# Loading the second row tile of x in two halves on two DMA queues: a change to the first microseconds of a long kernel

## The chip, the cores and the metric

The kernel runs on one core of one Trainium2 chip. The metric is device time in microseconds (us), lower is better. Before the change it was 921.45 us (median of three runs, 920.68 to 922.20). The profile of one execution gives a span from the first to the last instruction, here 919.1 us. The time of a run is longer than its span by what lies outside the instructions. The spans of most other runs are on record too, without a profile.

## The reference

One layer of a transformer, in bfloat16: normalise, sliding-window attention against cached keys and values, a SwiGLU network as a gate, and a residual.

```
x = A_x                                   # 1 x 2048 x 640
xn = _layernorm(x, axis=-1)
s = _A_ref(xn, A_k_cache, A_v_cache, A_wq, A_wo)      # 32 heads of 192, window of 512 keys
g = _silu(_B_ref(xn, B_w_gate, B_w_up, B_w_down))     # 640 -> 1536 -> 640
return x + s * g
```

## The kernel before

Only the opening matters here. The rows of x are worked on in tiles of 128. The first four tiles are normalised on VectorE and transposed on TensorE, each while TensorE multiplies the tile before it by the first three column blocks of the gate and up weights. From the fourth tile on TensorE has dense work, and the other 900 us follow.

The loads are issued from two queues, SP (`nc.sync`) and ACT (`nc.scalar`):

```python
def load_x(t, engs=(nc.sync,)):
    x_t[t] = lnx.tile([P, D], bf, name="x_t")
    n = P // len(engs)
    for k, eng in enumerate(engs):
        r = slice(k * n, (k + 1) * n)
        eng.dma_start(out=x_t[t][r, :], in_=x2[t * P + r.start : t * P + r.stop, :])
...
load_x(0, (nc.scalar, nc.sync))
load_x(1, (nc.scalar,))
load_first(slice(0, 2), (nc.sync, nc.scalar))     # gate on SP, up on ACT: input blocks 0, 1
load_first(slice(2, NC))                          # the rest of both, blocks 2 to 4, on SP
load_x(2, (nc.scalar,))
nc.scalar.activation(act_t[:], one_t[:], ACT.Sqrt)
load_x(3)
load_gu(1)
```

`load_first` loads 384 columns of the gate and of the up weights; I call its first part the first gate and up weights (192 KB each) and its second part the remaining ones (288 KB each). A row tile of x is 160 KB.

Two details of the order of work matter. While the loads are under way TensorE runs matmuls on zeros (`keep_warm`), which stand ahead of the real work in its queue until about 5.7 us. And the statistics of a tile are interleaved with the normalisation of the tile before it:

```python
ln_stats(0)
ln_sqrt(0)
ln_stats(1, lambda: ln_apply(0, (slice(0, 2 * P), slice(2 * P, D))))
ready(0)
...
            if k == len(order) * 7 // 10 and t < 3:
                if t < 2:
                    ln_stats(t + 2, lambda: ln_apply(t + 1))
                ...
                ready(t + 1)
```

`ln_stats(t, between)` calls `between` after the first half of tile t's statistics, so tile t - 1 is normalised only when tile t has landed. `ready` does the transposes. Of the matmuls of tile 0, the first part uses the gate weights only, then come the transposes of tile 1, then the remaining up weights.

The softmax here doesn't subtract the row's maximum and nothing guards it: scores larger than these inputs give would overflow.

## Time and profile before

| | before |
|---|---|
| median of 3 runs, us | 921.45 |
| span of the profiled run, us | 919.1 |
| TensorE busy | 914.2 us, 99% of the span |
| share of TensorE in the chain that ended last | 99% |
| start of the first dense matmuls, on tile gu | 14.38 us |

The last row is the yardstick. After it TensorE hardly stops, so whatever the opening gains or loses shows as a shift of that start: 919.1 - 14.38 = 904.7 us remain.

### The profile page before, as it was taken

What the parts mean: (1) busy time and instruction counts of PE and PEld (TensorE: products, weight loads), DVE (VectorE), ACT (ScalarE), POOL (GpSimd) and SP (SyncE); (2) the same over time, 40 slices, a digit from 0 to 9 for tenths busy, and PEclk for the clock granted to TensorE, in tenths of its full rate; (3) what the DMA queues carried; (4) which work ended last, traced back from release to release, by engine and by line L of the source; (5) the groups of instructions that cost most, each with busy time, mean ns of one, the idle gap of its engine ahead of it and who ended that gap; (6) DMA issues with size and microseconds to landing.
All of it is one profiled execution on the core that took longest, in us unless ns stands there. A gap on an engine that the chain in (4) does not pass through costs nothing.

```text
span 919.1 us, 23174 instructions
## 1 busy us (share of the span) xinstructions
PE 914.2 (99%) x9920; PEld 548.9 (60%) x9920; DVE 601.8 (65%) x844; ACT 473.9 (52%) x840; POOL 85.2 (9%) x269
## 2 busy tenths in 40 slices
PE   9999999999999999999999999999999999999998
PEld 6444444465757575656565656566666666665665
DVE  6443321467677777777777777676867777777657
ACT  4222222557464646565656565655555555556471
POOL 0000000000000000000000000000000000001976
PEclk9999999999999999999999999999999999999999
DMA  9412430045352534253534343435243444443525
GB/s 299 79 35 64 92 82 0 1 75 112 54 113 50 111 51 108 54 108 54 108 58 109 57 108 52 110 53 108 56 87 73 90 77 75 91 71 102 120 59 166
DMA packets 248167, 77.53 MB, mean 84 GB/s; under 512 B 228993, under 2 KB 248065, under 8 KB 248065
## 3 DMA queue, kind: packets, MB, share of 16 engines
q1 hardware_dynamic: 245696, 73.39, 38.9%
q10 hardware_dynamic: 2368, 2.67, 0.9%
q8 instruction: 77, 1.26, 0.6%
q14 instruction: 26, 0.20, 0.1%
HBM read 38.93 MB, written 2.62 MB: 45 GB/s over the span
## 4 chain that ended last, share of the span: by engine, by line
PE 99%; DMA 1%; DVE 0%; ACTq 0%; issue 0%
PE mm L448 22%; PE sc L462 18%; PE mm L487 16%; PE sc L602 15%; PE sc L282 11%; PE mm L312 6%; PE sc L572 4%; PE sc L564 2%; PE mm L539 2%; PE mm L564 1%; DMA x_t<-in_A_x_dram 1%; PE gu L282 0%; PE mm L321 0%; PE sc L487 0%; PE sc L539 0%; PE mm L462 0%
## 5 line engine op out<-in xcount | busy, mean ns | idle before, releaser
L466 ACT ACTIVATE p_t<-sc 128x1024 bf16<-128x1024 f32 x254 | 252.9, 1022 | 120.5 <-PE sc L462 120.5
L453 DVE TENSOR_REDUCE qT<-mm 128x512 bf16<-128x1024 f32 x189 | 231.1, 1223 | 99.0 <-PE mm L448 96.5
L517 ACT ACTIVATE O_b<-mm,r 128x192 bf16<-128x192 f32 x486 | 164.6, 421 | 183.7 <-issue 136.9
L448 PE MATMUL mm<-xnT,wq_p 64*128 64x512 bf16 x1890 | 237.5, 376 | 0.0
L462 PE MATMUL sc<-qT,khat 64*128 64x512 bf16 x1524 | 198.0, 376 | 0.0
L487 PEld LDWEIGHTS <-p_t 64*128 64x128 bf16 x3584 | 159.3, 93 | 33.8
L487 PE MATMUL mm<-V_p,p_t 64*128 64x193 bf16 x3520 | 176.7, 242 | 0.0
L615 DVE TENSOR_TENSOR s_m<-s_m,sc 128x1024 f32<-128x1024 f32 x108 | 131.9, 1221 | 60.7 <-PE sc L602 52.3
L602 PE MATMUL sc<-wo_p,OT_b 64*128 64x512 bf16 x1296 | 168.8, 376 | 0.0
L448 PEld LDWEIGHTS <-wq_p 64*128 64x128 bf16 x1890 | 105.0, 94 | 98.9 <-issue 0.8
L462 PEld LDWEIGHTS <-khat 64*128 64x128 bf16 x1536 | 85.3, 94 | 80.4 <-DVE s_t L615 0.3
L602 PEld LDWEIGHTS <-OT_b 64*128 64x128 bf16 x1296 | 70.1, 94 | 44.1 <-issue 0.3
L615 DVE TENSOR_TENSOR s_t<-s_t,sc 128x512 f32<-128x512 f32 x108 | 74.2, 687 | 28.4 <-PE sc L572 26.6
L589 POOL MEMSET turn_t<- 128x1 f32 x220 | 21.6, 98 | 700.2 <-PE mm L487 506.2
L290 DVE TENSOR_TENSOR hT<-sc,sg 128x512 bf16<-128x512 f32 x46 | 31.7, 692 | 81.5 <-ACT sg L289 81.5
L289 ACT ACTIVATE sg<-sc 128x512 bf16<-128x512 f32 x46 | 27.3, 596 | 69.8 <-PE sc L282 69.8
L282 PE MATMUL sc<-xnT,wu_sb 128*128 128x512 bf16 (+1 forms) x260 | 60.5, 355 | 0.0
L282 PE MATMUL sc<-xnT,wg_sb 128*128 128x512 bf16 (+1 forms) x260 | 60.3, 355 | 0.1
L572 PE MATMUL sc<-OT_b,wo_p 64*128 64x512 bf16 (+1 forms) x345 | 50.3, 376 | 0.0
L312 PE MATMUL mm<-wd_sb,hT 128*128 128x512 bf16 x192 | 43.9, 379 | 0.0
L282 PEld LDWEIGHTS <-wu_sb 128*128 128x128 bf16 x285 | 27.2, 98 | 26.8 <-issue 0.2
L282 PEld LDWEIGHTS <-wg_sb 128*128 128x128 bf16 x285 | 27.2, 98 | 26.3
(83 smaller groups left out, 418.8 us busy)
## 6 DMA issues: line engine op xcount, KB each, us to landing
wo_p<-in_A_wo_dram SPq DMA_DIRECT2D x16, 480.0 KB, 4.8
K_p<-in_A_k_cache_dram SPq DMA_DIRECT2D x32, 192.0 KB, 4.6
V_p<-in_A_v_cache_dram SPq DMA_DIRECT2D x32, 192.0 KB, 3.6
wq_p<-in_A_wq_dram SPq DMA_DIRECT2D x64, 80.0 KB, 2.9
wq_p<-in_A_wq_dram SPq DMA_DIRECT2D x16, 160.0 KB, 3.2
x_t<-in_A_x_dram SPq DMA_DIRECT2D x13, 160.0 KB, 3.2
x_b<-in_A_x_dram SPq DMA_DIRECT2D x4, 512.0 KB, 6.4
OT_b<-O_b SPq DMA_TRANSPOSE x124, 2.8
```

The source lines that it names most:

```text
L282: nc.tensor.matmul(out, w_sb[:, c, f * P : (f + 1) * P], xnT[:, c, qc], start=(c == 0), stop=(c == NC - 1),)
L290: nc.vector.tensor_tensor(hTs[b][:, f, :], u, sg[:], ALU.mult)
L312: nc.tensor.matmul(dn, at, by, start=(f == 0), stop=(f == NF - 1))
L448: nc.tensor.matmul(q_ps[:, h, :], pairs[pr]["wq"][r, c, j * P : (j + 1) * P], xnT[r, c, b * 512 : (b + 1) * 512], start=(c == 0), stop=(c ...
L453: nc.vector.reduce_sum(qTs[i][:, j, :], q_ps[:, :, :].rearrange("p h n -> p n h"), axis=AX.X)
L462: nc.tensor.matmul(sc[:, h, :], khat[r, j, ks], qT[r, j, :], start=(j == 0), stop=(j == 2))
L466: nc.scalar.activation(p_t[:, :, :], sc[:, :, :], ACT.Exp, scale=scale)
L487: m = nc.tensor.matmul(acc[:, k, h * 256 : h * 256 + Dh + 1], Ps[i][kc][r, h, qt * P : (qt + 1) * P], V_p[r, kc, h, 0 : Dh + 1], start=(p ...
L517: nc.scalar.activation(O_b[:, qt, h, :], a_k[:, h, 0:Dh], ACT.Copy, scale=r[:, k, h, :])
L572: nc.tensor.matmul(ps.rearrange("p (t q) -> p t q", q=P), pairs[i // NB]["wo"][r, j, MC:D], OTs[i][:, :, :].rearrange("p (t j) q -> p j t ...
L602: m = nc.tensor.matmul(ps[:, k, :], OTs[i][r, 3 * (2 * half + k) + j, :], pairs[i // NB]["wo"][r, j, MAIN], start=(turn == 0 and j == 0), ...
L615: nc.vector.tensor_tensor(to, to, ps, ALU.add)
```

## The change

The intent: tile 1 of x should arrive sooner, so that VectorE, and after it TensorE, can begin sooner.

```diff
         load_x(0, (nc.scalar, nc.sync))
-        load_x(1, (nc.scalar,))
+        load_x(1, (nc.scalar, nc.sync))
         load_first(slice(0, 2), (nc.sync, nc.scalar))
```

ACT then loads rows 0 to 63 of the tile and SP rows 64 to 127, ahead of the gate weights.

## The prediction

> **What bounds the kernel now.** I read the page from the top: busy time of each engine, then the chain that ended last, then that chain in order of time over the first 20 us (the only part that the change can touch), then the engines' timeline there.
>
> ```profile
> PE 914.2 (99%) x9920; PEld 548.9 (60%) x9920; DVE 601.8 (65%) x844; ACT 473.9 (52%) x840; POOL 85.2 (9%) x269
> ...
> PE 99%; DMA 1%; DVE 0%; ACTq 0%; issue 0%
> ```
>
> TensorE carries 99% of the chain, and its span is 919.1 us. All that is not TensorE work lies before the first dense matmuls. A change to the order of the first loads can at most win what the chain spends outside TensorE there. The chain in order of time shows how much that is (start, length, what):
>
> ```profile
> 1.33 0.59 ACTq L188
> 1.92 0.03 issue
> 1.95 0.45 ACTq L193
> 2.40 0.03 issue
> 2.43 4.79 DMA x_t<-in_A_x_dram
> 7.22 0.02 issue
> 7.24 0.49 DVE stats L243
> 7.74 0.07 DVE rstd L265
> 7.81 0.03 issue
> 7.83 0.46 DVE xn L267
> 8.29 0.05 issue
> 8.34 0.45 PE tp L335 x5
> ```
>
> So the start is bound by a load of x that is issued at 2.43 and lands at 7.22 us. By the order of the issues that is row tile 2, the fourth transfer of the ACT queue, not row tile 1, which the change splits. From 8.34 us on there is only TensorE in the chain. What row tile 1 itself costs is in VectorE's timeline (start, length, instruction, and in brackets the idle time before it):
>
> ```profile
> 4.87 0.49 DVE L243 BATCH_NORM_STATS2 stats<-x_t 128x6 f32<-128x320 bf16 x1 [0.29 <-DMA x_t<-in_A_x_dram]
> 5.28 0.15 DVE L265 RECIPROCAL rstd<-rstd 128x1 f32<-128x1 f32 x1
> 5.46 0.64 DVE L267 TENSOR_SCALAR xn<-x_t,mv,rstd 128x256 bf16<-128x256 bf16 x2
> ...
> 7.24 0.49 DVE L243 BATCH_NORM_STATS2 stats<-x_t 128x6 f32<-128x320 bf16 x1 [0.50 <-DMA x_t<-in_A_x_dram]
> ...
> 9.13 0.49 DVE L243 BATCH_NORM_STATS2 stats<-x_t 128x6 f32<-128x320 bf16 x1 [0.21 <-DMA x_t<-in_A_x_dram]
> ```
>
> There are three waits on x: 0.29 us for row tile 1, 0.50 for row tile 2, 0.21 for row tile 3. The first matters although row tile 0 is already there, because in program order the first half of tile t+1's statistics stands before the normalisation of tile t: tile 0 is held up by tile 1's load, tile 1 by tile 2's, tile 2 by tile 3's. TensorE's weight loads show what of this reaches it:
>
> ```profile
> 5.86 0.13 PEld L335 LDWEIGHTS <-xn 128*128 128x128 bf16 x2 [0.23 <-DVE xn L267]
> ...
> 8.33 0.28 PEld L335 LDWEIGHTS <-xn 128*128 128x128 bf16 x5 [0.23 <-DVE xn L267]
> ...
> 10.25 0.21 PEld L335 LDWEIGHTS <-xn 128*128 128x128 bf16 x3
> ```
>
> It waits 0.23 us before the transposes of tile 0 and 0.23 before those of tile 1. Before those of tile 2 (10.25) it has no wait to speak of, but little room either: in VectorE's timeline the normalised tile 2 is written from 9.73 to 9.73 + 0.45 = 10.18, only 0.07 earlier.
>
> **What the Trainium skill says.** "DMA: Bandwidth & Descriptors", section "Rules for kernel authors", says of two transfers to disjoint partition halves "Don't bother", because both use the same 16 engines. The trace can't refute that: in the issues of the first 0.7 us the two 80 KB halves of tile 0 landed after 2.3 and 2.6 us, the whole 160 KB of tile 1, behind one of them, after 3.5. The gain, if any, has to come from the order in the two queues and not from bandwidth. The same page, "Queues, rings and completion order", says that each DMA engine takes turns between the queues for which it has work. I use that below; the trace fits it loosely, for ACT's 592 KB in four transfers were all landed at 7.22 us while SP had also been served. "TensorE: Matmul & The Clock Gate", Part 1, says that the array starts at half clock and is released after a window of sustained work whose phase does not depend on the kernel, 107 ns against 56 ns between small matmuls. The trace agrees: weight loads for the first matmuls start at 6.78, 6.88, 6.99, 7.10, 7.20, 7.28 and from there 7.34, 7.39, 7.45, 7.50, that is 0.11 us apart and then 0.055. The full clock comes at about 7.28 us. The page's warning that this moment shifts from run to run would be a noise of some tenths of a microsecond; one trace can't show it.
>
> **The change part by part.** One 160 KB load on ACT becomes two of 80 KB, one on each queue. ACT issues as many as before (tile 0's half, tile 1's half instead of the whole, weights, tile 2). SP issues one more, before its first weights: SP's other half of tile 0 took 0.59 us to issue, so everything after it on SP is issued some 0.5 to 0.6 us later. No instruction of another engine is added or removed, and no byte: ACT's share of the opening falls from 80 + 160 + 192 + 160 = 592 KB to 512, SP's rises by 80.
>
> To say when something lands I count the bytes in front of it. In the stretches from 4.2 to 8.2 us the DMA moved 306, 316, 322 and 341 GB/s with its engines about fully busy, so 80 KB fewer in one's own queue, with the other queue taking equal turns, is some 160 KB fewer in all, or 160 x 1.024 / 320 = 0.51 us. Estimates, all from this trace:
> - Tile 1 lands now at 4.87 - 0.04 = 4.83 us. Its two halves, each second in its queue, should land at about 4.1. VectorE is free for it at 4.37 + 0.21 = 4.58, so the wait of 0.29 us goes and nothing takes its place there. Tile 0's normalised columns come 0.29 earlier, at about 5.5.
> - TensorE's transposes of tile 0 gain 0.23 us at most (its own wait), or somewhat less, since the warming matmuls before them end at about 5.7. The first real matmuls move from 6.72 to about 6.5. They then run at half clock until 7.28, so 0.2 us earlier is two matmuls more by then, worth 2 x 0.056 = 0.11 us.
> - Tile 2 has 80 KB fewer before it on ACT: 7.22 - 0.5 = 6.7 us. Its statistics can start at about 6.75 in place of 7.24, so normalised tile 1 is there at about 7.85 in place of 8.28, and TensorE's second wait of 0.23 goes. Together with the 0.11 TensorE is up to 0.3 us ahead at about 8 us.
> - The gate and up weights of the first two blocks: ACT's 192 KB come earlier; SP's land now at 1.37 + 4.3 = 5.67, and with 80 KB more before them at about 6.2. TensorE loads them at 6.34 now and would at 6.15. No wait, or 0.05. The rest on SP: gate at about 2.2 + 5.1 = 7.3, used at 7.56; up at 2.75 + 5.5 = 8.25, used at 8.57. For the up weights all 1,440 KB of both queues lie in front before and after, so they still land at about 8.25, just when a TensorE 0.3 us ahead would ask for them.
> - Tile 3, on SP: 3.27 + 5.8 = 9.07 us. In front of it and with it are 1,600 KB before and after the change, whatever the queue. It does not come earlier. Its statistics start at 9.13 as now, tile 2 is normalised at 10.18 as now, and the transposes of tile 2 can't begin before about 10.23. They begin at 10.25 now.
>
> So the 0.3 us that TensorE is ahead at 8 us is handed back at 10.2, in a wait for tile 2 which has no counterpart now. Sum: -0.11 - 0.23 + 0.28 = -0.06 us. After that every matmul follows the one before, and 0.05 us on the way stays 0.05 us at the end. Some straggling packets may well move by 0.1, so I take -0.1 us: 921.45 - 0.1 = 921.35.
>
> **The rivals.**
> First, the whole 0.3 us stays, because tile 3 comes earlier too. For it: with ACT's queue empty sooner SP runs alone for longer, and the stretch 8.2 to 9.2 us with SP alone moved 368 GB/s against 306 to 322 with both. Against it: the bytes are the same. It would make 921.1.
> Second, the weights become the bound: SP issues 0.5 to 0.6 us later, and from 3.2 to 4.2 us the engines were only 0.83 busy (202 GB/s), so the backlog isn't full there and a later issue may leave a gap. The first gate weights would hold the first matmuls to about 6.5 to 6.8, and the up weights land at 8.5 to 8.8. TensorE would then lose 0.2 to 0.3 us, with nothing after to win it back: 921.7. Against it: the added half of tile 1 fills just that gap on SP.
> Third, it is hidden altogether, since keep-warm matmuls stand in TensorE's queue to about 5.7 us: 921.45.
>
> **Range and chances.** All these lie within 0.3 us, or 0.03%. The three runs of before span 920.68 to 922.20, so the noise is larger than any of the effects, and it sets the range: 920.4 to 922.2. For 2% the change would need 18 us, while all waits on x in the opening sum to 1.0 us. Faster by over 2%: 0.01; within 2%: 0.98; slower by over 2%: 0.01.
>
> **What would show it.** Right: no wait of VectorE before the first statistics of tile 1 and a start near 4.58; first real matmul near 6.5; tile 2's load landing near 6.7; a new wait of 0.2 to 0.3 us before TensorE's transposes of tile 2; and start times of the dense matmuls (14.38 and 17.10 in the chain now) earlier by 0.0 to 0.1. Wrong: those starts earlier by 0.3, tile 3 landing well away from 9.07, or a wait for weights at 6.5 or 8.3 us. The prediction as a time fails only if the run-to-run noise is larger than three runs show.

## The result, and the profile after

The changed kernel took 920.96 us (median of six runs, 920.64 to 924.69), the kernel before 921.33 (median of six, 920.45 to 922.20). The ratio of the fast runs is 1.0004 with a 95% interval of 0.9987 to 1.002: the same (within 2%). A ratio here is the mean time of one kernel's fast runs over that of the other's in the same rounds, so it isn't quite the ratio of the medians: here the 924.69 pulls the mean up. Executions over 1.5% slower than the fastest of the same kernel are left out of the means.

The profiled execution happened to be that 924.69, with a span of 922.9 us. From its page, busy time and chain:

```profile
PE 914.9 (99%) x9920; PEld 551.6 (60%) x9920; DVE 601.7 (65%) x844; ACT 473.7 (51%) x840; POOL 85.2 (9%) x269
...
PE 98%; DMA 1%; SPq 0%; DVE 0%; issue 0%
```

TensorE's busy time is 0.7 us more than before, while the span is 3.8 us more. The chain in order of time (start, length, what) says where the rest is:

```profile
3.39 7.15 DMA wu_sb<-in_B_w_up_dram
10.53 0.05 issue
10.58 0.28 PE sc L282 x2
```

The chain no longer runs through tile 2 of x, but through the remaining up weights, which were issued at 3.39 and landed at 10.53 us. TensorE's weight loads in the same stretch (idle time and what ended it in brackets):

```profile
6.45 0.10 PEld L282 LDWEIGHTS <-wg_sb 128*128 128x128 bf16 x1 [0.41 <-DMA wg_sb<-in_B_w_gate_dram]
...
7.48 0.51 PEld L282 LDWEIGHTS <-wg_sb 128*128 128x128 bf16 x9 [0.36 <-DMA wg_sb<-in_B_w_gate_dram]
7.94 0.32 PEld L335 LDWEIGHTS <-xn 128*128 128x128 bf16 x5
10.58 0.51 PEld L282 LDWEIGHTS <-wu_sb 128*128 128x128 bf16 x9 [2.32 <-DMA wu_sb<-in_B_w_up_dram]
```

The transposes of tile 1 begin at 7.94 (8.33 before) and have no wait ahead of them any more. Three waits for weights are new: 0.41, 0.36 and 2.32 us. After the last of them the weight loads go at 11.13, 11.24, 11.35, 0.11 us apart, and stay at that pace to 14.4 us. The clock record of this trace says why: half the clock was granted from 11.04 us on for 3.41 us, and the view by stretches gives 0.52, 0.50 and 0.50 for 11 to 12, 12 to 13 and 13 to 14 us (the other profiles of this section and of the table below have no such stretch between the opening and the end). At half pace 3.41 us cost an estimated 1.7, so nearly half of the 3.8 us is the clock after the late load, and not the wait itself. VectorE's statistics of tiles 1, 2 and 3:

```profile
4.59 0.49 DVE L243 BATCH_NORM_STATS2 stats<-x_t 128x6 f32<-128x320 bf16 x1
...
6.38 0.44 DVE L243 BATCH_NORM_STATS2 stats<-x_t 128x6 f32<-128x320 bf16 x1
...
11.04 0.49 DVE L243 BATCH_NORM_STATS2 stats<-x_t 128x6 f32<-128x320 bf16 x1 [2.79 <-DMA x_t<-in_A_x_dram]
```

The waits for tiles 1 and 2 are gone, and one of 2.79 us for tile 3 has come. So this trace shows what the change was meant to do and a loss many times larger; yet four of the other five runs were at or under 921.05. One profile doesn't tell what belongs to the change and what to the run. The experiments had to settle that first.

### The profile page after: what moved, and what is told of

Its sections match the earlier page's. It is cut to its first block, busy times and chain, and to the rows that moved or that the text cites. A ratio compares the mean times of both kernels' runs of the same rounds, so it can differ in the third digit from the quotient of the medians.

```text
span 922.9 us, 23176 instructions
## 1 busy us (share of the span) xinstructions
PE 914.9 (99%) x9920; PEld 551.6 (60%) x9920; DVE 601.7 (65%) x844; ACT 473.7 (51%) x840; POOL 85.2 (9%) x269
## 3 DMA queue, kind: packets, MB, share of 16 engines
q10 hardware_dynamic: 2304, 2.59, 0.9%
## 4 chain that ended last, share of the span: by engine, by line
PE 98%; DMA 1%; SPq 0%; DVE 0%; issue 0%
PE mm L448 22%; PE sc L462 18%; PE mm L487 16%; PE sc L602 15%; PE sc L282 11%; PE mm L312 6%; PE sc L572 4%; PE sc L564 2%; PE mm L539 2%; DMA wu_sb<-in_B_w_up_dram 1%; PE mm L564 1%; PE gu L282 0%; PE mm L321 0%; PE sc L487 0%; PE sc L539 0%; SPq L188 0%
```

## The experiments

Two theories. A (chance): in each execution some load is late, whichever kernel it is; the late up weights are such a case. B (the change): the extra transfer on SP makes SP's later loads late. And one question behind both: in which order do the DMA engines serve what the two queues have issued?

### Repeats of both kernels

No edit; each run gives one more profile and five more times.

> The changed kernel, not altered, profiled a second time. Theory A (chance): the 2.3 us in which TensorE waited for the remaining up weights in the first profile was one late transfer, not a property of the change; now the up weights land near 8.3 us, the wait for them is under 0.3 us, the span is near 919 us and the first dense matmul on tile gu (14.38 us in the chain of the kernel before) starts between 14.1 and 14.5. Theory B (the change pushes SP's weights too late): the wait for the up weights is there again, at least 0.5 us, and the span is at least 920 us. Time ratio to the kernel before under A 0.9995 to 1.0000, under B 1.001 to 1.003.

> The kernel before, not altered, against itself: how far two profiles of one kernel differ. Theory A: its loads land up to 1 us apart from the first profile's, and the moment at which matmuls go from 107 to 56 ns apart moves by up to 3 us; dense start between 13.5 and 16 us; all of the difference in span is made before 20 us. Theory B: it repeats the first profile to 0.2 us (span 919.1, dense start 14.4). Time ratio 1.000 within 0.0005.

> The changed kernel once more, for another profile of its opening: in the two so far tile 3's last packets landed after 10 us, in the two of the kernel before under 9.2 us. Theory A (chance among the DMA engines): in at least one of this and the next repeat, up weights and tile 3 land under 9.3 us, the dense start on tile gu is 14.0 to 14.6 us, span 918.8 to 919.3. Theory B (the change makes the later SP loads late): both repeats show TensorE or VectorE waiting at 8 to 11 us for up weights or tile 3 by 1 us or more, dense start after 15 us. Time ratio under A 0.9995 to 1.0003, under B 1.0005 to 1.002.

> The kernel before once more, the control to the repeats of the changed one. Theory A: one of its profiles may as well show a load over 1 us late, and where none does the dense start is 14.3 to 14.8 us, as in the two so far. Theory B: tile 3 lands under 9.3 us and no wait for weights appears, as in both so far. Time ratio 1.000 within 0.0005.

> As after_3, the second repeat. Theory A: its late loads, if any, are not the same ones as in the first profile; dense start 14.0 to 14.6 us if none is late. Theory B: up weights and tile 3 after 10 us again. And for the prediction's step on tile 3: where no load is late, TensorE waits 0.2 to 0.3 us before the transposes of tile 2, and the dense start is within 0.1 us of the kernel before.

> The changed kernel, a last repeat. So far TensorE waited for the remaining up weights by 2.32 and 1.31 us in two of its three profiles at full clock, in none of the three of the kernel before. If that belongs to the change (chance 2 in 3 or so each time), the wait is there again by over 0.5 us and the dense start is after 14.8; if it was luck, no such wait and a dense start of 14.1 to 14.3. In both cases tile 2's load lands at 6.2 to 6.6 us (7.2 to 7.6 before) and tile 1's at 4.5 to 5.0. Time ratio 0.999 to 1.001.

Measured. The landings are the issue times plus the times to landing of the DMA issues, in us, both rounded, so that a landing can be 0.1 off; "dense" is the start of the first dense matmuls on tile gu, "wait up" TensorE's wait for the remaining up weights.

| profile | tile 1 | tile 2 | first gate | rest of gate | rest of up | tile 3 | wait up | dense | span |
|---|---|---|---|---|---|---|---|---|---|
| before | 4.8 | 7.2 | 5.7 | 7.3 | 8.3 | 9.1 | 0 | 14.38 | 919.1 |
| before_2 | 4.9 | 7.6 | 6.1 | 7.3 | 8.3 | 8.7 | 0 | 14.77 | 919.5 |
| before_3 | 3.9 | 7.2 | 5.9 | 7.3 | 8.2 | 8.7 | 0 | 14.34 | 919.1 |
| changed | 4.5 | 6.2 | 6.4 | 7.5 | 10.5 | 11.0 | 2.32 | 17.97 | 922.9 |
| after_3 | 5.0 | 6.4 | 5.9 | 7.3 | 8.2 | 8.7 | 0 | 14.21 | 919.1 |
| after_4 | 5.0 | 6.5 | 6.0 | 7.7 | 9.8 | 10.3 | 1.31 | 15.64 | 920.6 |
| after_5 | 4.5 | 6.3 | 5.7 | 7.5 | 8.4 | 8.9 | 0 | 14.16 | 919.1 |

The profile of after_2 is left out of the table: it fell in a run of 2507.18 us, in which TensorE was too slow to wait for anything; its clock is told at the end. Its loads were late too: the rest of up landed at 3.40 + 6.5 = 9.9 us.

The times: after_2 922.19 us (median; ratio 1.0008, interval 0.9994 to 1.0021), after_3 921.06 (0.9993, 0.998 to 1.0005), after_4 921.81 (1.0000, 0.9986 to 1.0013), after_5 921.15 (0.9993, 0.9981 to 1.0005). The kernel before against itself: before_2 921.12 (1.0002), before_3 921.96 (1.0001). Every interval contains 1. All fast runs of these jobs and the first one together are 25 of the changed kernel with a mean of 921.55 us and 45 of the kernel before with 921.59.

What follows:
- Span minus dense start is 904.7 to 905.0 us in every row. All differences in span above 0.3 us arise in the opening.
- A difference below that does not, and it takes back the gain. ScalarE's activation no. 810, at 892 us, still starts 0.22 us (after_5) and 0.17 us (after_3) earlier than in the first profile of before; yet the spans are 919.07 and 919.14 against 919.12. What is lost, 0.17 to 0.19 us, is lost at the very end, where SP waits for the stores of the output. The sum, number and longest of these waits from 912 us on, first in before and then in after_5:

```profile
SPq L853 <- DMA out_dram<-x_b: 1.2, 3, 0.6
```

```profile
SPq L853 <- DMA out_dram<-x_b: 1.4, 1, 1.4
```

  In before the store that lands last is also the last to be checked, at 918.3 us. In after_5 one check waits for it for 1.4 us, to 918.09, and three more checks, already fulfilled, follow 0.06 us apart. This order is in all seven profiles at full clock in which SP and ACT together issue one load more than before (also in x1_swap, x1_late and up_act below), and in none of the six others. Why the order changes with the number of loads isn't shown.
- Tile 2 lands at 6.2 to 6.5 us instead of 7.2 to 7.6 in all profiles of the changed kernel. That belongs to the change, as far as four profiles go; x1_swap and x1_late below don't have it.
- Tile 1 does not land earlier: 4.5 to 5.0 against 3.9 to 4.9. What the change was made for, it doesn't do.
- The late up weights are in two of four profiles of the changed kernel and in none of three of the kernel before. Theory B as I wrote it ("both repeats") has fallen with after_3; theory A isn't shown either, since the kernel before never had one. Seven profiles are too few (and so are eight with after_2), and whether the change makes this one load late more often stays open. The spans say more than the times: all fast runs of the changed kernel have a mean span of 919.46 us (25 runs, 3 of them at 920.0 or more, the longest 922.9), those of the kernel before whose span is on record 919.45 (39 runs, 8 at 920.0 or more, the longest 921.4, in the run of 924.29 us). So executions that lose about 1 us or more are no rarer without the change, though no profile of such a one of the kernel before was kept, and what was late there isn't known. This speaks for theory A as to the cost, without showing it.
- What "late" means can be seen in the packets of the traces. A row of x is one packet of 1280 bytes, and tile 3 stands right behind the up weights in SP's queue. In the profiles of table rows without a late load all 128 rows of tile 3 had been started by 8.7 us. In the first profile of the changed kernel 120 had by then, and the last 8 start between 10.12 and 10.48, 0.05 us apart; in after_2 the last 8 start between 9.53 and 9.90, in after_4 the last 16 between 9.32 and 9.78, in pairs. Eight rows are one sixteenth of the tile, so it looks as if one of the 16 DMA engines, or two, had fallen behind while the others were on time. The packed trace doesn't name the engine, and the reason isn't shown.
- Where nothing is late, the dense start is 14.16 and 14.21, against 14.34, 14.38 and 14.77. This is a gain of 0.1 to 0.2 us over the two better profiles of before, against a spread of 0.4 among those of before alone; and by the second point above it doesn't reach the end of the span.

What binds the changed kernel when nothing is late is in the chain of after_5, which is to be compared with the line `2.43 4.79 DMA x_t<-in_A_x_dram` of before:

```profile
2.88 4.63 DMA wg_sb<-in_B_w_gate_dram
```

The remaining gate weights have taken the place of tile 2 as the load that is waited for last. TensorE's wait for them before its loads at about 7.5 us is 0.36, 0.34 and 0.39 us in three of the four profiles; in after_3 there is none, and the chain there begins with tile 1 (landed at 5.02). The kernel before has such a wait too where TensorE starts early: 0.26 us in before_3, whose tile 1 landed at 3.9. VectorE in after_5, tiles 2 and 3:

```profile
6.35 0.45 DVE L243 BATCH_NORM_STATS2 stats<-x_t 128x6 f32<-128x320 bf16 x1
...
8.97 0.49 DVE L243 BATCH_NORM_STATS2 stats<-x_t 128x6 f32<-128x320 bf16 x1 [0.62 <-DMA x_t<-in_A_x_dram]
```

VectorE has a wait of 0.62 us for tile 3, as the prediction wanted it, but the profile names no wait of TensorE for it: the transposes of tile 2 begin at 10.06 and the chain runs on TensorE without a break from 7.51 us. TensorE, held up by gate weights, isn't far enough ahead to feel tile 3.

### Tile 3 on a third queue

```diff
-        load_x(3)
+        load_x(3, (nc.gpsimd,))
```

> The changed kernel with row tile 3 loaded from GpSimd's queue in place of SP's fifth transfer. If tile 3's landing is what takes back the gain (the prediction's step): tile 3 lands before 7 us, VectorE has no wait before its statistics, TensorE no wait before the transposes of tile 2, and dense matmuls start 0.2 to 0.3 us earlier than in the changed kernel where no other load is late; time ratio 0.9996. If the weights bind instead: TensorE waits for gate or up weights at 6.5 to 8.5 us by 0.2 us or more, the dense start does not move, ratio 1.000.

Measured: 923.85 us (ratio 1.0022, interval 1.0009 to 1.0035), slower than the kernel before by some 2 us. VectorE has no wait for tile 3 any more (its statistics start at 8.92), so tile 3 doesn't bind there. But TensorE's weight loads read:

```profile
8.70 0.51 PEld L282 LDWEIGHTS <-wg_sb 128*128 128x128 bf16 x9 [0.96 <-DMA wg_sb<-in_B_w_gate_dram]
```

The remaining gate weights landed at 2.89 + 5.77 = 8.66 instead of 7.3 to 7.7 us, with 160 KB more in front of them. The second expectation held for the wait, and with it the claim that to load one tile earlier is to load another later; it failed for the dense start, which moved to 15.37, and for the ratio. Span 920.6. The span explains 1.5 us of the time; this run was 3.25 us longer than its span, other profiled runs 1.8 to 2.9, so a part of the loss lies outside the instructions. The five spans are 920.1 to 922.4.

### Tile 1 whole on SP

```diff
-        load_x(1, (nc.scalar, nc.sync))
+        load_x(1)
```

> Row tile 1 not in halves but whole on SP, as SP's second transfer: this keeps the move of bytes off ACT's queue and takes away the split. If only the order in the queues counts, tile 1 lands near 4.6 to 4.9 us (160 KB behind 80), tile 2 earlier than in the changed kernel (432 KB on ACT in place of 512: near 6.0), and SP's first gate weights some 0.5 us later still, so TensorE waits for them by 0.3 to 0.6 us before the first matmul; time ratio 1.0003. If the split itself counts, tile 1 lands after 5 us and VectorE's wait of 0.3 us or more before its statistics is back.

Measured: 921.36 us (ratio 1.0003, interval 0.9989 to 1.0016). Tile 1 landed at 1.38 + 4.20 = 5.58, and VectorE's statistics of it read:

```profile
5.60 0.49 DVE L243 BATCH_NORM_STATS2 stats<-x_t 128x6 f32<-128x320 bf16 x1 [1.09 <-DMA x_t<-in_A_x_dram]
```

That is over 5 us with a wait of more than 0.3, the sign that I had written down for "the split itself counts". By itself this is weak: whole on ACT the tile lands at 3.9 to 4.9, so SP against ACT makes as much of a difference as the split. The split merely avoids the worst of the three arrangements. No load was late (up weights at 3.21 + 5.1 = 8.3), although SP carried 80 KB more than in the changed kernel. The wait for the first gate weights that I expected did not come: by the time that tile 0 was normalised they had landed. Tile 2 landed at 1.95 + 3.9 = 5.8, near the 6.0 that I expected. Dense start 14.72.

### The halves exchanged

```diff
-        load_x(1, (nc.scalar, nc.sync))
+        load_x(1, (nc.sync, nc.scalar))
```

> The changed kernel with the two halves of tile 1 exchanged between the queues, everything else equal. The amount and order of bytes on each queue are the same. If the late up weights come from the order and load of the SP queue, they are late here as often; if from which rows each queue carries, up weights land near 8.3 us. One run can only speak against the second by being late. Dense start 14.1 to 14.3 if nothing is late. Time ratio 0.999 to 1.001.

Measured: 921.37 us (ratio 0.9993, interval 0.9980 to 1.0006). Tile 1 landed at 4.3, tile 2 at 7.0, gate rest at 7.6, up weights at 8.5; dense start 14.34, span 919.2. Nothing late, so as the expectation says it can't tell; the spans of all five runs, 918.9 to 919.2, have no late opening either. It does show that tile 2's gain isn't sure: it landed at 7.0 with the same bytes on each queue.

### SP's half of tile 1 after the first gate weights

```diff
-        load_x(1, (nc.scalar, nc.sync))
+        x_t[1] = lnx.tile([P, D], bf, name="x_t")
+        nc.scalar.dma_start(out=x_t[1][0:64, :], in_=x2[P : P + 64, :])
         load_first(slice(0, 2), (nc.sync, nc.scalar))
+        nc.sync.dma_start(out=x_t[1][64:P, :], in_=x2[P + 64 : 2 * P, :])
```

> The changed kernel with SP's half of tile 1 issued after SP's first gate weights instead of ahead of them. If what SP pays is the wait for its first gate weights (0.41 us in the first profile of the changed kernel), that wait goes, the gate weights land near 5.7 us as in the kernel before, tile 1 lands at 4.5 to 5.0 us and VectorE waits 0 to 0.4 us for it; dense start as in the kernel before within 0.3 us, time ratio 0.9995 to 1.0005. If it is only the bytes on SP that count for the late loads, up weights and tile 3 land after 10 us as in the changed kernel.

Measured: 923.84 us (ratio 1.0018, interval 1.0006 to 1.0031). The first gate weights came early, at 1.38 + 3.2 = 4.6 us, and tile 1 late, at 2.23 + 3.56 = 5.79:

```profile
5.89 0.49 DVE L245 BATCH_NORM_STATS2 stats<-x_t 128x6 f32<-128x320 bf16 x1 [1.32 <-DMA x_t<-in_A_x_dram]
```

The expected 0 to 0.4 us of wait were 1.32, and the dense start is at 15.00. The exchange of two neighbouring issues on one queue moved the one load 1.1 to 1.8 us forward and the other 0.8 to 1.3 back. The wait of 0.41 us for the gate weights went, at the price of 1.32 us for tile 1. By the second part of the expectation nothing was late in this profile: the up weights landed at 8.9, tile 3 at 9.4. Tile 2 landed at 2.60 + 4.9 = 7.5. The profile fell in the fastest of the five runs, with a span of 919.9; the four others have 921.2 to 922.4, at mean clocks of 0.997 and 0.998, and what they lost beyond the wait shown is not profiled.

### The remaining up weights on ACT, with and without the change

```diff
-        load_first(slice(2, NC))
+        src = B_w_gate[2 * P : D, 0:FQ].rearrange("(c p) f -> p c f", p=P)
+        nc.sync.dma_start(out=wg_sb[:, 2:NC, 0:FQ], in_=src)
...
         ln_sqrt(0)
+        src = B_w_up[2 * P : D, 0:FQ].rearrange("(c p) f -> p c f", p=P)
+        nc.scalar.dma_start(out=wu_sb[:, 2:NC, 0:FQ], in_=src)
```

> The changed kernel with the remaining up weights issued on ACT, after the first square root (about 4.8 us), in place of SP. If the lag is SP's ring alone after ACT's has run dry, up weights land at 7.8 to 8.5 us, tile 3 (288 KB less before it on SP) at 7.5 to 8.3, TensorE has no wait for either, dense start 14.0 to 14.25, time ratio 0.9990 to 0.9998. If the bytes bind whatever the queue, up weights or tile 3 are late by over 0.5 us here too, ratio 1.000 or more.

> The same move of the up weights in the kernel before (tile 1 whole on ACT). If the split has a gain of its own that the late up weights hid, this one is 0.1 to 0.2 us behind the last kernel: tile 2's load still lands at 7.2 to 7.6 us, VectorE waits 0.5 to 0.9 us for it, dense start 14.3 to 14.8. If the split has none, both have the same dense start within 0.1 us. Time ratio 1.000 within 0.0007.

Measured: 925.98 us with the change (ratio 1.0039, interval 1.0024 to 1.0054) and 927.34 without (1.0057, 1.0045 to 1.0069). Both are clearly slower than the kernel before, and in their profiles by the very wait that they were to remove: TensorE waits 2.23 and 3.87 us for the up weights. In the second the clock record has 3.41 us at half the clock from 12.56 on as well, an estimated 1.7 us. The first profile fell in the fastest of its six runs (span 921.3, the others 922.5 to 925.2). The chains, first with and then without the change:

```profile
4.57 6.02 DMA wu_sb<-in_B_w_up_dram
10.58 0.04 issue
```

```profile
4.63 7.62 DMA wu_sb<-in_B_w_up_dram
12.25 0.05 issue
```

ACT's queue had nothing else to do after tile 2 had landed (6.5 and 7.0 us), and the 288 KB still took until 10.58 and 12.25. If the engines had taken equal turns from the issue on, I would estimate 288 x 1.024 x 2 / 320 = 1.8 us for them. The packets show where the time went. SP's queue is q1, ACT's q10; packets, MB and share of the 16 engines from 8 to 9 us in the run with the change:

```profile
q10 hardware_dynamic: 264, 0.20, 60.2%
q1 hardware_dynamic: 217, 0.16, 48.1%
```

There ACT's queue moved more than SP's. But from 6.2 to 7.0 us, about 2 us after the issue, it had moved nothing, and SP's 0.26 MB. So the transfer began late and then shared. Without the change ACT's queue moved nothing from 7 to 8 us and most of the 288 KB from 9 to 11.

The landings of the two runs tell the same, with the reserve that it is one profile of each and that tile 1 is split in one only. Up to the moment of ACT's issue SP had issued one of the two 480 KB loads of the next weights with the change (3.91; the other at 4.97), and both without (3.27 and 3.90). That is 480 KB less in front of ACT's transfer, and it landed 12.25 - 10.59 = 1.66 us earlier: 480 x 1.024 / 1.66 = 296 GB/s, about the rate of the opening (306 to 341 GB/s from 4.2 to 8.2 us before). So the landings are nearly those of service in the order of issue, as if the queues were one row; what holds the later transfer back is not shown. The guess of the expectation, that "SP's ring alone" was slow, has fallen.

No version beat the kernel before by more than the noise.

## Why the prediction was right or wrong

The time was right: 921.35 predicted, 920.96 measured, within the range of 920.4 to 922.2, and the class was "same". It is right for the reason that carries the class (all waits on x in the opening sum to 1.0 us of 921). The forecast of -0.1 us itself is smaller than the noise and can't be confirmed by the times; that 920.96 lies below 921.33 is luck, since over all fast runs the means are 921.55 and 921.59. Several inner steps were wrong, and that their sum comes out near the forecast is luck as well.

**"Tile 1's two halves should land at about 4.1": wrong.** They landed at 4.5 to 5.0. VectorE's first wait went in two profiles (starts at 4.59 and 4.56) and stayed in two (0.57 and 0.43 us). The first real matmul was thus no sure 0.2 us earlier. The Trainium skill, "DMA: Bandwidth & Descriptors", "Rules for kernel authors", had the rule for it: the halves run on the same engines, so they aren't faster than the whole. I quoted it and then counted with a gain all the same. The issue was dearer than counted, too: SP's half of tile 1 took 0.81 us to issue, and SP's later loads were issued 0.64 to 0.87 us later, not 0.5 to 0.6.

**"80 KB fewer in one's own queue is some 160 KB fewer in all": wrong as a model, and it was the step under tile 2's size.** I expected tile 2 at 6.7 us by equal turns. It landed at 6.2 to 6.5, 0.7 to 1.4 us earlier than before in place of 0.5. In the order of issue it would be plain: before, the 288 KB of remaining gate weights are issued at about 2.2, ahead of tile 2 (2.43); after, SP's extra issue moves them to 2.88, behind tile 2 (2.60). 288 x 1.024 / 296 = 1.0 us. By this reading the gain isn't the lighter ACT queue but a neighbour's later issue. The experiment with the up weights and x1_sync (tile 2 issued at 1.95, the remaining gate weights at 2.70, landed at 5.8) support it. x1_swap and x1_late, with tile 2 issued at 2.60 ahead of the remaining gate weights and landed at 7.0 and 7.5, don't fit it and are unexplained. So it is argued, not shown.

**"TensorE's second wait of 0.23 goes": right where it counts.** Before the transposes of tile 1 it was 0.23, 0.80 and 0.42 us in the three profiles of before. In the changed kernel it is 0.17 or none, and the transposes begin at 7.94 to 8.24 in place of 8.29 to 8.71.

**"They run at half clock until 7.28": true of that one trace only.** In all other profiles of table 1 the first real weight loads go 0.055 us apart from the start (before_2: 6.62, 6.68, 6.73). The clock records agree: the first one at full clock begins at 7.23 us in before and between 4.2 and 6.1 in the others. The Trainium skill, "TensorE: Matmul & The Clock Gate", Part 1, warns that the moment varies from run to run; these traces agree, and it was not to be counted with.

**"Handed back at 10.2, in a wait for tile 2": not shown.** In after_3 tile 3 landed at 8.7 and TensorE did not wait; in after_5 VectorE waited 0.62 us for tile 3, and TensorE did not. In two others tile 3 was over 1 us late, together with the up weights. The 0.1 to 0.2 us that TensorE has at the transposes of tile 1 are still there at the dense start. Nearest to the forecast comes x1_swap: VectorE waited 0.47 us for tile 3, the transposes of tile 2 took 0.36 us in the chain in place of 0.28, and the dense start is 14.34, as in before_3. What was handed back in after_3 and after_5 was handed back at the end of the program, in SP's waits for the stores, so "0.05 us on the way stays 0.05 us at the end" held to 892 us and not beyond. What kept the gain small was the wait for the remaining gate weights, 0.34 to 0.39 us in three of four profiles; in the fourth, after_3, tile 1 came late (5.02) and was the bound. The prediction had put these at 7.3 us with TensorE asking at 7.56, and left open by how much TensorE's head start would run into them. That is the second rival in a small form: the weights did become the bound. The third rival, the warming matmuls, shows as a floor: the transposes of tile 0 begin at 5.58 without a wait in after_5 and also in before_3, and nowhere earlier.

**"Up weights land at about 8.25": right in after_3 and after_5 (8.2, 8.4), wrong in two (9.8, 10.5).** Why is open, as said above.

**The range: right.** It was set by the noise, not by the effect. The noise was somewhat wider than three runs showed: 920.45 to 924.29 for the kernel before, 920.64 to 924.69 for the changed one.

## What to carry to other kernels

Where loads at the start already filled the DMA engines, splitting one of them didn't make it come sooner here; it changed who stood before whom. Write the loads of both queues in one row by their time of issue, with bytes, and ask for each at what time its user wants it: an extra issue on one queue pushes back the issue of everything behind it there (by 0.64 to 0.87 us here) and may let the other queue's next load pass (it did in four profiles of the changed kernel, and not in x1_swap). Look at the end of the program too, even for a change to its start. And before a profile of a change of some tenths of a microsecond is explained, take a second one of both kernels: here the first of the changed kernel showed a loss of 3.8 us that its next repeat at full clock did not have. Compare the spans of all runs as well.

## What the Trainium skill lacked or had wrong

- "DMA: Bandwidth & Descriptors", "Queues, rings and completion order": each engine is said to take turns between the queues for which it has work. Once ACT's packets ran, the queues did share (0.20 MB against 0.16 from 8 to 9 us). But 288 KB alone on ACT, issued at 4.57 us behind SP's earlier loads, moved nothing from 6.2 to 7.0 us and took 6.02 us to land, and 7.62 us with 480 KB more issued before it on SP, where equal turns from the issue on would be an estimated 1.8 us. The page gives nothing by which one could have foreseen this late begin; the runs don't show its mechanism.
- The same page gives no spread of one transfer's landing over executions of one program. The 288 KB of remaining up weights, issued at 3.38 to 3.40 us each time, landed after 4.8, 5.0, 6.4, 6.5 and 7.1 us.
- "TensorE: Matmul & The Clock Gate", Part 1, names a half clock and a reduced clock for many cores. One execution of the changed kernel took 2507.18 us, correct in its result, with the groups of instructions saying

```profile
L448 PE MATMUL mm<-xnT,wq_p 64*128 64x512 bf16 x1890 | 610.4, 832 | 0.0
```

  where the last but one column is the mean of one in ns: 832 against 376 before. The mean clock of 1.00 listed for it is no reading: this trace holds no clock record at all, and the tool then counts nothing as lost. That the clock was low is therefore an inference from the matmuls. The page mentions a clock stuck low for tens of microseconds; here the slow pace held for the whole run. One of 26 runs of the changed kernel and none of 45 of the kernel before had it, too few to tie it to the change. A mean over all runs would have been ruined by it.
- No page gives the time between this metric and the span of the program's own instructions (the overheads listed in "Runtime: NRT & Kernel Launch" are defined otherwise). Here it was 1.74 to 3.48 us over the fast runs of both kernels and varied by 0.9 us between three profiles of the kernel before (1.98, 2.59 and 2.86), more than the whole effect studied.
- No page speaks of the order in which a program's end checks the stores of its output. Here one load more in the opening went with a different order of these checks and 0.17 to 0.19 us at the end.
